# One run of probability-value matmuls per step instead of three, with scratch tiles shared

## The chip, the cores and the metric

The kernel runs on one core of a Trainium2 chip. The metric is the device time of one execution in microseconds (us), lower is better. The engines are named as the profile names them: PE is TensorE's matmuls, PEld its weight loads, DVE is VectorE, ACT is ScalarE, POOL is GpSimd, SP is the engine that issues the DMAs.

## The reference

Top-32 attention over 4 batches, 8 heads, 576 positions of 64 values, then two feed-forward layers over all 2304 tokens:

```
scores = (q @ k.T) / sqrt(64)                  # per batch and head, 576 x 576
scores = where(scores >= 32nd largest of the row, scores, -1e9)
attn   = softmax(scores) @ v                   # heads side by side: x, 2304 x 512
x = (sigmoid(x @ w_gate) * (x @ w_val)) @ w_out        # 512 -> 1536 -> 512
h = x @ w_in                                           # 512 -> 1024
out = layernorm(h * softmax(h)) * g_ln @ w_out2        # 1024 -> 512
```

All inputs are float32.

## The kernel before, in words

Attention is cut into 72 steps. 64 of them are main steps: 128 query rows of one head pair of one batch. 8 are remainder steps, which hold the last 64 rows of two head pairs. Four steps fill one chunk of 128 tokens (18 chunks), and each chunk then goes through the two feed-forward layers.

One step runs like this. TensorE makes the scores (`scores`, L607), ScalarE copies them out (L614), VectorE searches the top 32 with max and match-replace (L635, L639), ScalarE and GpSimd mask and exponentiate (L668, L672, L677), GpSimd scales the rows (L694). The probabilities then have to be turned: `flip` (L704) transposes the step's nine 128x128 blocks in three groups of 4, 4 and 1 blocks through the one PSUM tile with tag `pt`; `take_flip` (L711 for batch 0, L714 otherwise) copies a group to SBUF on ScalarE, and for batches 1 to 3 `rest_flip` (L719) writes the low half of the numbers on VectorE (tile `et`, two float16 parts). `attend` (L739) multiplies the group with the values: the stationary operand is a 128x64 block of values, the moving one 128 probabilities, and the output is one half (64 partitions) of the chunk's PSUM tile `av`. Batch 0 is done with one float32 matmul per block, the others with three float16 ones. A main step has 30 such float16 matmuls (12, 12 and 6 by group) or 10 float32 ones (4, 4 and 2 matmuls by program; the profile shows each float32 matmul as two instructions: 8, 8 and 4). All other matmuls of the kernel have a stationary operand of 128 columns.

The feed-forward layers of a chunk are `gate` and `value` (L886, 12 groups of 12 matmuls each), `down` (L932, 12 groups of 12), a norm (`norm2`, L938: ScalarE squares `px` into a scratch tile that nobody reads, only its sum is used), `hidden` (L969, 8 groups of 3 matmuls of 512 columns), layer norm, `turn` (L1041, transposes) and `last` (L1067, 8 groups of 3). Between them ScalarE writes a float32 copy of a result into a tile with tag `xf` (one buffer: `xf`, `xg`, `lf`, 64 times in all), and GpSimd reads it to make a low half (L778, L959, L1058).

At the start VectorE rebuilds the weights from 64-bit words (L411 to L418). For one matrix ScalarE squares its 12 pieces (`square`, L425, scratch tag `sq`). `norm_v` (L585) squares the 16 value tiles (scratch tag `sj`, which `norm2` uses too).

The order of all work on every engine is fixed before the kernel is emitted. Class `Order` holds operations with engine, cost, rank, needs and the buffers they take and free, and plays a list schedule with them; the rank of an operation is its due time plus the sums of `SHIFT` entries, a table of some 400 numbers. On the chip each engine runs its own list strictly in that order. `BUFS` says how many buffers each tag has. In the planner, one `at` operation stands for one call of `attend`, with costs of 0.36, 0.36 and 0.18 us for the three groups of a float16 step.

Of the kernel before, what the change touches and what calls it, by code (L numbers as in the profile page):

```python
# [43 lines left out]
BUFS = dict(s=4, ks=8, v=4, qr=3, qs=3, w=2, et=3, eu=2, ps=1, pt=1, av=1, pm=4, xt=1, gh=1, two=3, big=2, xf=1, sq=1, x2=1)  # L44
# [263 lines left out]
def body(ctx, tc, q_main, q_rem, k_dup, v_pad, w_gate, w_val, w_out1, w_in, w_out2, g_ln, out):  # L308
# [72 lines left out]
    def weights(key, dst, src, kk, nn, by_column=False, fold=None):  # L381
# [41 lines left out]
        def square(f, c):  # L423
            state["sq", f, c] = sq = tl(sp, [P, 512], BF16, "sq", "sq")
            nc.scalar.activation(sq, piece(f, c), AF.Square)  # L425
# [373 lines left out]
    for i, st in enumerate(steps):  # L799
# [49 lines left out]
        for g in parts:  # L849
# [5 lines left out]
            elif i and not st["first"]:  # L855
                needs.append(("at", i - 1, 2))
# [354 lines left out]
```

## Time and profile before

| | us |
|---|---|
| median of the runs (3) | 1113.74 |
| lowest and highest | 1113.10 and 1115.08 |
| the profiled execution's own time | 1114.34 |
| its span, first to last instruction | 1112.2 |
| mean granted TensorE clock in it | 0.958 |

The times of the steps come from the profiled execution, which took 2.1 us more than its span and 0.6 us more than the median. "Busy" of PE is modelled: matmuls overlap in the pipeline, so that what a group of matmuls costs is the distance from its start to the start of the next group.

### The profile page before, as it was taken

The numbers are of one execution on the slowest core, as the hardware profiler recorded it, in microseconds if no ns is written. First come the engines' busy times: TensorE is split into PE (matmuls) and PEld (weight loads), VectorE is DVE, ScalarE is ACT, GpSimd is POOL, SyncE is SP. The second block draws the span as 40 slices with busy tenths as digits, with TensorE's granted clock in tenths as the row PEclk, the third lists the DMA queues.
The fourth block names the chain that finished last, engine by engine and source line by source line (L and its number), as shares of the span: only waits on it lengthen the run. The fifth ranks groups of instructions, "written<-read, shape, count | busy, mean of one in ns | idle before, by whom it ended". The sixth has DMA issues, their size and how long they took to land.

```text
span 1112.2 us, 31341 instructions
## 1 busy us (share of the span) xinstructions
PE 984.1 (88%) x12500; PEld 796.3 (72%) x12500; DVE 977.8 (88%) x2888; ACT 826.1 (74%) x1561; POOL 701.1 (63%) x940
## 2 busy tenths in 40 slices
PE   1536837699999999999999999999999999999995
PEld 1324835488786877887878787887977797887962
DVE  8998999999799999998999999996999999995232
ACT  2697599977888877786889677778798786766331
POOL 3555487967887677668688675667687566564100
PEclk9975869899999999999999999999999999999998
DMA  9844331011220000012100000012200000000000
GB/s 323 282 133 161 103 129 54 1 35 42 79 73 17 16 12 26 22 48 59 57 32 9 23 12 21 25 38 89 68 16 11 26 12 6 12 11 11 2 11 19
DMA packets 29474, 59.16 MB, mean 53 GB/s; under 512 B 3984, under 2 KB 14224, under 8 KB 29328
## 3 DMA queue, kind: packets, MB, share of 16 engines
q1 hardware_dynamic: 29328, 57.16, 15.7%
q8 instruction: 98, 1.61, 0.6%
q14 instruction: 48, 0.39, 0.1%
HBM read 52.43 MB, written 4.72 MB: 51 GB/s over the span
## 4 chain that ended last, share of the span: by engine, by line
PE 55%; ACT 18%; DVE 15%; POOL 5%; DMA 4%; issue 3%; SPq 0%; POOLq 0%; ACTq 0%
PE pg L886 10%; PE px L932 9%; PE pv L886 8%; PE po L1067 7%; PE ph L969 6%; PE av L739 5%; DVE m L635 5%; PE pt L704 5%; PE ps L607 4%; DVE w L639 4%; DMA kr<-in_k_dup_dram 2%; ACT s L677 2%; ACT w L668 2%; ACT ts L472 2%; ACT s L614 1%
## 5 line engine op out<-in xcount | busy, mean ns | idle before, releaser
L635 DVE MAX8 m<-w 128x8 f32<-128x576 f32 (+1 forms) x576 | 338.6, 602 | 2.8
L639 DVE MATCH_REPLACE8 w<-m,w 128x288 f32<-128x288 f32 (+1 forms) x432 | 233.9, 543 | 0.0
L672 POOL TENSOR_TENSOR s<-s,w 128x576 f32<-128x576 f32 x144 | 203.3, 1419 | 40.3 <-ACT w L668 39.4
L932 PE MATMUL px<-gh,wo 128*128 128x128 f16 x2592 | 178.8, 220 | 0.5 <-POOL gh L920 0.5
L932 PEld LDWEIGHTS <-wo 128*128 128x128 f16 x2592 | 157.2, 99 | 24.0 <-issue 1.7
L886 PE MATMUL pg<-xt,wg 128*128 128x128 f16 x2592 | 169.0, 221 | 3.1 <-DVE jk L438 1.4
L886 PE MATMUL pv<-xt,wv 128*128 128x128 f16 x2592 | 166.5, 219 | 1.0 <-DVE wi L418 1.0
L886 PEld LDWEIGHTS <-wv 128*128 128x128 f16 x2592 | 151.7, 98 | 16.6 <-issue 2.3
L607 PE MATMUL ps<-ks,qs 128*128 128x288 f32 x640 | 129.1, 330 | 38.4 <-DVE w L625 18.9
L886 PEld LDWEIGHTS <-wg 128*128 128x128 f16 x2592 | 154.1, 99 | 11.5 <-issue 2.8
L668 ACT ACTIVATE w<-s,ed 128x576 f32<-128x576 f32 x144 | 120.4, 864 | 31.1 <-POOL ed L663 30.8
L607 PEld LDWEIGHTS ps<-ks,qs 128*128 128x128 f32 x640 | 96.4, 198 | 51.3 <-issue 14.5
L704 PE MATMUL pt<-ident,s 128*128 128x128 f32 x648 | 115.4, 287 | 15.2 <-ACT et L711 8.7
L969 PE MATMUL ph<-wi,x 128*128 128x512 f16 x432 | 122.4, 394 | 3.0 <-ACT x L949 2.2
L1067 PE MATMUL po<-wo,lt 128*128 128x512 f16 x432 | 120.8, 392 | 2.0 <-ACT lf L1050 2.0
L677 ACT ACTIVATE s<-s,nm 128x576 f32<-128x576 f32 x144 | 111.3, 774 | 14.0 <-POOL s L672 13.3
L714 ACT ACTIVATE et<-pt 128x512 f16<-128x512 f32 (+1 forms) x162 | 78.6, 485 | 53.7 <-PE pt L704 46.4
L614 ACT ACTIVATE s<-ps 128x576 f32<-128x576 f32 x144 | 93.0, 646 | 28.7 <-PE ps L607 25.5
L694 POOL TENSOR_SCALAR s<-s,sm 128x576 f32<-128x576 f32 x132 | 97.4, 746 | 24.7 <-DVE sm L686 17.6
L719 DVE SCALAR_TENSOR_TENSOR et<-pt,et 128x512 f16<-128x512 f32 (+1 forms) x162 | 89.0, 549 | 24.1 <-ACT et L714 23.2
L739 PE MATMUL av<-et,v 128*64 128x128 f16 (+3 forms) x2200 | 107.7, 234 | 0.6 <-ACT et L711 0.5
L704 PEld LDWEIGHTS pt<-ident,s 128*128 128x128 f32 x648 | 76.8, 145 | 40.7 <-ACT et L711 15.3
(179 smaller groups left out, 1668.5 us busy)
## 6 DMA issues: line engine op xcount, KB each, us to landing
kr<-in_k_dup_dram SPq DMA_DIRECT2D x16, 576.0 KB, 4.0
qr<-in_q_main_dram SPq DMA_DIRECT2D x64, 128.0 KB, 2.5
v<-in_v_pad_dram SPq DMA_DIRECT2D x16, 320.0 KB, 3.4
wi<-in_w_gate_dram SPq DMA_DIRECT2D x8, 512.0 KB, 5.2
wo<-in_w_val_dram SPq DMA_DIRECT2D x8, 512.0 KB, 6.3
raw<-in_w_in_dram SPq DMA_DIRECT2D x8, 512.0 KB, 3.7
wi<-in_w_out_dram SPq DMA_DIRECT2D x8, 512.0 KB, 4.3
raw<-in_w_out_dram SPq DMA_DIRECT2D x8, 512.0 KB, 3.3
```

Source lines behind the costliest of these rows:

```text
L607: nc.tensor.matmul(pt[:, nn, :S // 2], qs[:, hl, slot], ks[:, nn * (S // 2):(nn + 1) * (S // 2)], start=x == 0, stop=x == len(mm) - 1)
L635: nc.vector.max(st["m8"][:, t, r * 8:r * 8 + 8], ranked(i, r, t))
L639: nc.vector.match_replace(w, steps[i]["m8"][:, t, r * 8:r * 8 + 8], w, LOW)
L668: nc.scalar.activation(st["w"][:, t], st["s"][:, t], AF.Relu, bias=st["ed"][:, 1, t:t + 1], scale=st["ed"][:, 0, t:t + 1])
L672: nc.gpsimd.tensor_sub(st["s"][:, t], st["s"][:, t], st["w"][:, t])
L677: nc.scalar.activation(w, w, AF.Exp, bias=st["nm"][:, t:t + 1], scale=D ** -0.5, accum_out=st["sm"][:, t:t + 1])
L704: nc.tensor.transpose(pt[:, x], wf[:, k * P:(k + 1) * P], ident)
L739: nc.tensor.matmul(ch["av"][j * D:(j + 1) * D, p, st["o"]:st["o"] + wd], v, e[:, y * REM:y * REM + wd], start=one and k == (0, 5)[j], stop ...
L886: nc.tensor.matmul(dst, w[a][:, c, f * P:(f + 1) * P], ch["xt"][:, b, c], start=x == 0, stop=x == len(mm) - 1)
L932: nc.tensor.matmul(ch["px"][:, e], wo1h[a][:, f, e * P:(e + 1) * P], ch["gh"][:, b, f], start=y == 0, stop=y == len(DOWN) - 1)
L969: nc.tensor.matmul(ch["ph", nn], ch["x2"][:, a, c], wih[b][:, c, nn * 512:(nn + 1) * 512], start=c == 0 and a == 0 and b == 0, stop=c == K ...
L1067: nc.tensor.matmul(ch["po"], ch["lt"][:, a, f], wo2h[b][:, f], start=y == 0, stop=y == len(FIN) - 1)
```

## The change

`attend` is called once per step and multiplies all nine blocks, in the same order of blocks and terms as before. In the planner its operation needs all three groups of the step, and frees their buffers together; its cost is 1.06 us for a float16 main step. The first group of a step takes both `et` buffers of the step at once, and `et` grows from 3 buffers to 4. To make room, the scratch tags `sq` and `sj` go: `square` writes into the buffer of tag `x2` (one buffer, the input of `hidden`), `norm_v` and `norm2` into that of tag `xf`. The `SHIFT` table is replaced as a whole.

```diff
-BUFS = dict(s=4, ks=8, v=4, qr=3, qs=3, w=2, et=3, eu=2, ps=1, pt=1, av=1, pm=4, xt=1, gh=1, two=3, big=2, xf=1, sq=1, x2=1)
+BUFS = dict(s=4, ks=8, v=4, qr=3, qs=3, w=2, et=4, eu=2, ps=1, pt=1, av=1, pm=4, xt=1, gh=1, two=3, big=2, xf=1, x2=1)
...
-    ("m", "first"): -68.8, ("r", 0): 592.7, ("r", "first"): -187.5, ("m", 1): -2148.3, ("r", 1): -823.6,
...
+    ("m", "first"): -17.1, ("r", 0): 598.7, ("r", "first"): -174, ("m", 1): -2556.4, ("r", 1): -732.5, ("m", 2): 8.4,
...
-            state["sq", f, c] = sq = tl(sp, [P, 512], BF16, "sq", "sq")
+            state["sq", f, c] = sq = tl(sp, [P, 512], BF16, "sq", "x2")
...
-        sq = tl(sp, [P, NBLK + 1, D], BF16, "sqv", "sj", 1)
+        sq = tl(sp, [P, NBLK + 1, D], BF16, "sqv", "xf")
...
-    def attend(i, g):
+    def attend(i):
...
-        blocks = range(NBLK) if st["rem"] else range(4 * g, min(4 * g + 4, NBLK))
...
-                      for x in blocks for j in range(2)]
+                      for x in range(NBLK) for j in range(2)]
...
-                      for x0 in range(0, len(blocks), 2) for n, (a, c) in enumerate(TERMS) for x in blocks[x0:x0 + 2]
-                      for j in range(2)]
+                      for x0 in range(0, NBLK, 2) for n, (a, c) in enumerate(TERMS)
+                      for x in range(x0, min(x0 + 2, NBLK)) for j in range(2)]
...
-        add(("vn", b, p), "ACT", 0.75, t + STEP, lambda b=b, p=p: norm_v(b, p), [("vd", b, p)])
+        add(("vn", b, p), "ACT", 0.75, t + STEP, lambda b=b, p=p: norm_v(b, p), [("vd", b, p)], take=["xf"], free=["xf"])
...
-            add(("et", i, g), "ACT", (0.49, 0.49, 0.17)[g], e + 6, lambda i=i, g=g: take_flip(i, g), [("fl", i, g)], take=[ET[g]],
+            add(("et", i, g), "ACT", (0.49, 0.49, 0.17)[g], e + 6, lambda i=i, g=g: take_flip(i, g), [("fl", i, g)] + [("et", i, g - 1)] * (g > 0),
+                take=(["et"] * 2, [], ["eu"])[g],
...
-        parts = (2,) if rem else range(3)
-        for g in parts:
-            whole = b in WHOLE
-            needs = [("et" if whole else "ez", i, x) for x in (range(3) if rem else [g])]
...
+        whole = b in WHOLE
+        needs = [("et" if whole else "ez", i, x) for x in range(3)]
+        needs += [n for p in st["pairs"] for n in ([("vd", b, p)] if whole else [("vl", b, p, x) for x in range(2)])]
+        needs += [("at", i - 1)] * (i > 0 and not st["first"])
+        add(("at", i), "PE", 1.41 if whole else 1.18 if rem else 1.06, e + 6, lambda i=i: attend(i), needs,
+            take=["av"] if st["first"] else [],
+            free=list(ET) + ["v"] * sum(uses[b, p][-1] == i for p in st["pairs"]))
...
-        sq = tl(sp, [P, 512], BF16, "sq2", "sj", 1)
+        sq = tl(sp, [P, 512], BF16, "sq2", "xf")
...
-        op(("n2",), "ACT", 0.57, 43, lambda ch=ch: norm2(ch), [("do", x, 11)])
+        op(("n2",), "ACT", 0.57, 43, lambda ch=ch: norm2(ch), [("do", x, 11)], take=["xf"], free=["xf"])
```

## Rows read from the trace of the kernel before

**Rows 1.** The page, part 1: busy time of each engine, its share, instructions.

```profile
PE 984.1 (88%) x12500; PEld 796.3 (72%) x12500; DVE 977.8 (88%) x2888; ACT 826.1 (74%) x1561; POOL 701.1 (63%) x940
```

**Rows 2.** Busy time by stretch: us, each engine (instructions), PEclk, DMA share, GB/s.

```profile
0.00:200.00 200.00, 105.29 (x894) 80.31 (x894) 186.32 (x485) 150.58 (x253) 115.77 (x128) 0.82 0.49 165
200.00:350.00 150.00, 138.70 (x1771) 117.83 (x1772) 140.03 (x437) 124.33 (x243) 116.47 (x161) 0.98 0.14 44
350.00:1008.00 658.00, 649.48 (x8800) 532.28 (x8799) 619.81 (x1892) 514.00 (x1003) 457.74 (x634) 1.00 0.09 28
1008.00:1037.00 29.00, 29.00 (x383) 22.16 (x380) 8.83 (x18) 12.84 (x21) 4.84 (x7) 1.00 0.03 11
1037.00:1112.20 75.20, 61.59 (x662) 43.77 (x659) 22.80 (x60) 24.31 (x44) 6.30 (x12) 0.93 0.03 12
...
350.00:500.00 150.00, 149.33 (x2048) 121.66 (x2046) 145.09 (x448) 121.48 (x237) 104.63 (x149) 1.00 0.08 25
```

**Rows 3.** Groups by form, line 739: busy us, mean ns, idle before.

```profile
L739 PE MATMUL av<-et,v 128*64 128x128 f16 x1440 | 66.9, 224 | 0.0
...
L739 PEld LDWEIGHTS <-v 128*64 128x64 f16 x1800 | 50.7, 110 | 28.6 <-issue 20.3 <-ACT tv L592 0.4 <-ACT v L593 0.2
...
L739 PE MATMUL av<-et,v 128*64 128x128 f32 x320 | 31.1, 324 | 0.6 <-ACT et L711 0.5
```

**Rows 4.** TensorE's timeline near 1022 us: start, us, what, count.

```profile
1022.24 0.83 PE L886 MATMUL pv<-xt,wv 128*128 128x128 f16 x12
1023.00 0.53 PE L739 MATMUL av<-et,v 128*64 128x128 f16 x12
1023.46 0.84 PE L886 MATMUL pv<-xt,wv 128*128 128x128 f16 x12
1024.23 0.36 PE L739 MATMUL av<-et,v 128*64 128x128 f16 x6
1024.53 0.66 PE L704 MATMUL pt<-ident,s 128*128 128x128 f32 x4
...
1026.24 0.84 PE L886 MATMUL pv<-xt,wv 128*128 128x128 f16 x12
1026.92 0.84 PE L969 MATMUL ph<-wi,x 128*128 128x512 f16 x3
```

**Rows 5.** TensorE's timeline: one of the two runs of 24 matmuls.

```profile
734.62 0.86 PE L739 MATMUL av<-et,v 128*64 128x128 f16 x24
735.42 0.84 PE L886 MATMUL pg<-xt,wg 128*128 128x128 f16 x12
```

**Rows 6.** TensorE's timeline: first and last runs of line 739, float32, then float16.

```profile
205.94 1.10 PE L739 MATMUL av<-et,v 128*64 128x128 f32 x8
...
299.19 0.44 PE L739 MATMUL av<-et,v 128*64 128x128 f32 x4
...
371.19 0.53 PE L739 MATMUL av<-et,v 128*64 128x128 f16 x12
...
1037.12 0.36 PE L739 MATMUL av<-et,v 128*64 128x128 f16 x6
```

**Rows 7.** Waits of ScalarE, by cause: us in total, times, longest.

```profile
ACT et L714 <- PE av L739: 7.0, 4, 3.2
...
ACT xg L953 <- POOL lt L1058: 1.3, 2, 0.7
...
ACT lf L1050 <- POOL lt L1058: 0.8, 1, 0.8
```

**Rows 8.** Timelines of PE, DVE and ACT: four instructions, idle in brackets.

```profile
843.24 1.44 PE L886 MATMUL pg<-xt,wg 128*128 128x128 f16 x23 [0.69 <-POOL xt L778]
...
1008.24 0.15 DVE L657 TENSOR_SCALAR ed<-ed 128x1 uint32<-128x1 uint32 x1
...
1037.53 0.60 ACT L761 ACTIVATE xt<-av 128x512 f16<-128x512 f32 x1 [8.82 <-PE av L739]
...
1099.58 1.94 PE L1041 MATMUL pl<-ident,e 128*128 128x128 f32 x8 [8.10 <-DVE e L1033]
```

More of the change, by code (lines that the diff above doesn't have):

```diff
@@ L161, in terms @@
     own += [((k, "first"), 1.0)] * (name[1] < 18) + [((k, "end"), 1.0)] * (name[1] > 63)
-    return [((k, name[2]) if k in ("m", "r", "fl", "et", "ez", "at") else k, 1.0), (("A", name[1] // 4), 1.0)] + own
+    return [((k, name[2]) if k in ("m", "r", "fl", "et", "ez") else k, 1.0), (("A", name[1] // 4), 1.0)] + own
 class Order:
@@ L175 @@
     TAKER = dict(s="ACT", ks="POOL", v="DMA", qr="DMA", qs="POOL", w="DVE", et="ACT", eu="ACT", ps="PE", pt="PE", av="PE", pm="PE",
-                 xt="ACT", gh="ACT", two="ACT", big="DMA", xf="ACT", sq="ACT", x2="ACT")
+                 xt="ACT", gh="ACT", two="ACT", big="DMA", xf="ACT", x2="ACT")
     WINDOW, TABLE, FIRST, BACK = 3413, 1280, 1650, 150
@@ L489, in weights @@
             if by_column:
-                add(("wq", *W), "ACT", 0.52, t, lambda f=f, c=c: square(f, c), [("wr", *W)], take=["sq"])
+                add(("wq", *W), "ACT", 0.52, t, lambda f=f, c=c: square(f, c), [("wr", *W)], take=["x2"])
                 add(("wp", *W), "PE", 0.22, t, lambda f=f, c=c: columns(f, c),
-                    [("wq", *W)] + [("wp", key, f, c - 1)] * (c > 0), take=["pm"] if c == 0 else [], free=["sq"])
+                    [("wq", *W)] + [("wp", key, f, c - 1)] * (c > 0), take=["pm"] if c == 0 else [], free=["x2"])
                 if c == kk - 1:
@@ L847, in body @@
                 add(("ez", i, g), "DVE", (0.6, 0.6, 0.2)[g], e + 6, lambda i=i, g=g: rest_flip(i, g), [("et", i, g)], free=["pt"])
-        parts = (2,) if rem else range(3)
-        for g in parts:
-            whole = b in WHOLE
-            needs = [("et" if whole else "ez", i, x) for x in (range(3) if rem else [g])]
-            needs += [n for p in st["pairs"] for n in ([("vd", b, p)] if whole else [("vl", b, p, x) for x in range(2)])]
-            if g != parts[0]:
-                needs.append(("at", i, g - 1))
-            elif i and not st["first"]:
-                needs.append(("at", i - 1, 2))
-            add(("at", i, g), "PE", (1.35 if whole else 0.9) if rem else (0.69, 0.69, 0.46)[g] if whole else (0.36, 0.36, 0.18)[g], e + 6, lambda i=i, g=g: attend(i, g), needs,
-                take=["av"] if st["first"] and g == parts[0] else [],
-                free=list(ET if rem else ET[g:g + 1]) + ["v"] * (g == 2) * sum(uses[b, p][-1] == i for p in st["pairs"]))
+        whole = b in WHOLE
[5 more added lines that the diff above has]
+            free=list(ET) + ["v"] * sum(uses[b, p][-1] == i for p in st["pairs"]))
         if st["last"]:
@@ L867, in body @@
                           free=["pt"])
-            needs = [("at", i, 2), ("ve", key)]
+            needs = [("at", i), ("ve", key)]
             for bb in ch["vs"]:
```

142 rows, old and new, of the table SHIFT are left out of this document.

## The prediction

> **What bounds the kernel now.** I read the page first: over the whole span TensorE and VectorE are busy alike, 88% each [rows 1], so the average names no bound. The table of stretches does more [rows 2]. Up to 200 us TensorE is busy for 105 of 200 us while VectorE is for 186: there VectorE sets the pace (it rebuilds weights and searches the first top 32). From 350 to 1008 us TensorE is busy for 649.5 of 658 us, with a granted clock of 1.00: it idles 8.5 us, VectorE 38.2 us. The top-32 search ends at 1008.2 us [rows 8]. In the 29 us behind it TensorE has no idle time at all, and in the last 75.2 us it is busy for 61.6 [rows 2], the largest hole being the 8.1 us before the last transposes [rows 8]. So TensorE works off a queue from 350 us on, and that queue is still there when the search is over. The sign of this is ScalarE's wait of 8.8 us at 1037.5 us for the last run of `av` matmuls [rows 8]: other matmuls stood before it in TensorE's list. A microsecond taken from TensorE after 350 us should thus shorten the kernel, as long as VectorE can follow.
>
> **What a run of `av` matmuls costs.** The listed busy times don't say it, since matmuls overlap: line 739 shows 224 ns for one float16 matmul [rows 3]. I take distances between starts in the timeline [rows 4]. A group of 12 `pv` matmuls followed by other full-width matmuls takes 0.68 us (1026.24 to 1026.92). The same group followed by `av` takes 0.76 or 0.77 us (1022.24 to 1023.00, 1023.46 to 1024.23): entering the run costs 0.09, say 0.10. A run of 12 `av` matmuls takes 0.46 us to the next start, a run of 6 takes 0.30. The difference of 6 matmuls is 0.16 to 0.17, or 0.028 each, so 12 matmuls are 0.34 and 0.12 us is left that depends on no matmul: leaving the run. A run of 24 confirms the line: 0.80 us [rows 5] against 24 x 0.028 + 0.12 = 0.79. So every run costs 0.22 us on top of its matmuls. The weight loads show the same from their side: 28.6 us of idle time before those of line 739, mostly under "issue", which is no wait for another engine [rows 3].
>
> **Part 1, one run instead of three.** The matmuls stay: 1440 of float16 in main steps, 320 of float32 [rows 3]. Only runs go. Between the first and the last run of the float16 main steps [rows 6] I counted 139 runs, without the remainder steps' (48 steps x 3, less 5 places where two already stand together). After it 48 are left: 91 x 0.22 = 20.0 us of TensorE's time. Bounds: 10.9 if a merged run still pays the entering somewhere (91 x 0.12), 20.9 at 0.23 per run, the top of the readings. A merged run of 30 comes to 0.10 + 0.84 + 0.12 = 1.06 us; before, the three are 0.56 + 0.56 + 0.40 = 1.52.
>
> The float32 steps after 200 us have 26 runs [rows 6] for 10 steps: 16 x 0.22 = 3.5 us at the most. TensorE is not full there (138.7 of 150 us from 200 to 350 [rows 2]), so I take half, 1.8; lower bound 0, upper 3.5. Before 200 us I take nothing: TensorE idles half of that time, and VectorE's 186 us cover it. The remainder steps are one run already and stay.
>
> **How much of it arrives.** VectorE's 619.8 us from 350 to 1008 [rows 2] don't shrink. Its fullest long stretch, 350 to 500 us, is 145.1 of 150, or 96.7% [rows 2]. At that share the 658 us can become 619.8 / 0.967 = 641, so the search could end 17 us earlier. The rest can come out of the tail: a chunk's own groups on TensorE are 36 of about 0.67 us and 16 of about 0.68 [rows 4], 35 us, of the 61.6 busy behind 1037 us; some 26 us there are older chunks' work. Both routes together hold more than 20 us. Against that, TensorE waits a dozen times between 350 and 1008 us, the last cluster ending at 843.2 us [rows 8], where it had caught up; time saved just before such a wait is lost in it. My estimate is that 85% of 21.8 arrives: 18.5 us.
>
> A rule of the Trainium skill (Perfetto Trace Analysis, Identifying the Most-Contended Engine) speaks against this. It says that matmul busy time is no measure of TensorE's load and that the busy share of weight loads is to be taken. By it TensorE stands at 532.3 / 658 = 81% from 350 to 1008 us [rows 2], VectorE at 94% would be the most contended, and the sum would be that of the first rival below. The timeline agrees with it only that the busy figure is padded; starts that follow each other without a gap show a full list.
>
> **Part 2, buffers.** Three `et` buffers become four, taken in pairs. ScalarE waits for `av` matmuls to free an `et` 4 times for 7.0 us now [rows 7]. A pair is held until the step's one run, but two steps fit instead of one and a half; I take 0, between -7 (those waits go) and +3.2 (one more of the longest). The run now comes after the third group's low half, so 30 instead of 6 matmuls stand behind the last group of a chunk: 24 x 0.028 = 0.7 us later for ScalarE's copy. This is covered by other chunks' matmuls except at the last chunk, so I charge 0.7 once; without that cover it would be 18 chunks, 12 us.
>
> **Part 3, shared scratch.** `square` takes the buffer of `x2`, which nobody needs before the first chunk's second layer: 0. `norm_v` (16 times) and `norm2` (18 times) now need the single `xf`, so ScalarE may stand until GpSimd has read the copy before. Behind it on ScalarE wait the score copies and `et` copies, and for those wait TensorE and VectorE. Today's 64 users of `xf` wait 1.3 + 0.8 = 2.1 us altogether [rows 7], 0.033 each; 34 more give 1.1 us, of which I let 0.2 through, since ScalarE is busy for only 514 of 658 us [rows 2]. Bounds: 0, and 34 x 0.7 (the longest such wait) = 24 us.
>
> **Part 4, the replaced table.** It moves work on all queues, DMA issues on SP's included, by amounts that the trace of before cannot show. I take 0; the bounds are what order alone can give or take: the 8.5 us in which TensorE idles from 350 to 1008 us [rows 2], gained or doubled.
>
> Sum on the profiled execution's 1114.3: -18.5 + 0.7 + 0.2 = -17.6, or 1096.7. The median of the runs is 0.6 lower, so 1096.
>
> **The rivals.** First, VectorE sets the pace: attention doesn't speed up, TensorE only idles longer up to the cluster of waits that ends at 843 us, and what counts is saved behind it. By then 16 of the 48 steps are left, with 46 runs: 30 x 0.22 = 6.6 us, or 1107. For it speaks VectorE's 94%; against it that VectorE idles 38 us in that stretch and that the queue outlives the search. Chance 0.20. The rule of the Trainium skill named above (Perfetto Trace Analysis) would have it this way.
>
> Second, the gain is eaten at each step: the merged run sits in TensorE's list where VectorE's third low half isn't done, and waits some 0.4 us per step (48 x 0.4 = 19). Today TensorE hardly waits at `av`: 0.6 us of idle at its float32 runs, 0.0 at the float16 ones [rows 3]. 1113.7; chance 0.09.
>
> Third, slower: `xf`. The place is ScalarE's squares at L938 and L585. Each stands until GpSimd has finished the copy before. It decides against the change when the 34 waits cost the path over 0.52 us each (17.6 / 34). At the longest wait seen, 0.7, it is 24 - 17.6, about 6 us above: 1120. Against it: the same buffer causes 0.033 us per use now [rows 7]. Chance 0.13, in which I include the replaced table going wrong at the batch changes at the same price.
>
> **Numbers.** The forecast has 0.58, with its own range of 1088 to 1103. A change of 0.2% (2.2 us) is about what the runs can tell from none. Faster by more: 0.58 + 0.20 = 0.78; within: 0.09; slower: 0.13. The range takes the forecast and the first rival. Its lower end is all of 20.0 + 3.5, and some 5 of the idle time or of the `et` waits: 1114.3 - 29 = 1085. Its upper end is 1110, the first rival with only 4 us left.
>
> **What would show it.** Right: 48 float16 runs of 30 with 0.95 to 0.97 us from their start to the next, TensorE still above 97% from 350 us to the end of the search, the search ending before 1000 us, and VectorE at 96% or more. Wrong: the search still ending near 1008 us with more TensorE idle (first rival); idle time before `av` for VectorE's low halves (second); ScalarE's squares waiting for GpSimd by tens of microseconds (third). The forecast fails as a whole if a merged run costs more per matmul than 0.028.

## The result, and the profile after

| | before | after |
|---|---|---|
| median of the runs, us | 1114.41 | 1099.56 |
| lowest to highest, us | 1113.10 to 1117.45 | 1097.92 to 1101.90 |
| the profiled execution: time, span, us | 1114.34, 1112.2 | 1101.90, 1100.1 |

The ratio is 0.9864, with a 95% interval of 0.9836 to 0.9893: 14.9 us faster. A second measurement of the changed kernel, beside the last experiments, gave 1099.91 us and 0.9869 (0.9851 to 0.9888). The profiled execution of after is the slowest of its four runs.

Part 1 of the page of the changed kernel, busy time of each engine:

```profile
PE 970.6 (88%) x12500; PEld 801.8 (73%) x12500; DVE 971.5 (88%) x2888; ACT 827.8 (75%) x1561; POOL 701.2 (64%) x940
```

Again both shares are 88%, as in [rows 1], and again they name no bound. By line and form, line 738 (739 before), with busy us, mean ns and the idle time in front:

```profile
L738 PE MATMUL av<-et,v 128*64 128x128 f16 x1440 | 49.2, 221 | 0.0
...
L738 PEld LDWEIGHTS <-v 128*64 128x64 f16 x1800 | 48.0, 110 | 10.1 <-issue 7.0 <-POOL v L597 0.3
```

Their count is that of [rows 3] and their mean about the same, but TensorE is busy with them for 17.7 us less, and the idle time before their weight loads fell from 28.6 to 10.1 us: 18.5 us, close to the 20.0 that the prediction had counted from 91 runs. In the timeline 139 runs became 46, so 93 went: 44 runs of 30 matmuls are left, and two of 60, where two steps stand together. One of the two, and one of the 44 between its neighbours (start, us, what, count):

```profile
380.20 1.87 PE L738 MATMUL av<-et,v 128*64 128x128 f16 x60
...
444.61 0.84 PE L881 MATMUL pv<-xt,wv 128*128 128x128 f16 x12
445.39 1.03 PE L738 MATMUL av<-et,v 128*64 128x128 f16 x30
446.35 0.66 PE L704 MATMUL pt<-ident,s 128*128 128x128 f32 x4
```

The group of 12 in front takes 0.78 us to the run's start (0.67 where no run follows), and the run of 30 takes 0.96 us to the next start. The median over such runs is 0.96.

The stretches, cut at the new end of the search (us, busy PE, PEld, DVE, ACT, POOL, with instruction counts, then PEclk, DMA share, GB/s):

```profile
200.00:350.00 150.00, 142.63 (x1800) 121.11 (x1799) 138.16 (x440) 130.98 (x252) 119.73 (x158) 0.98 0.13 42
350.00:993.00 643.00, 630.28 (x8721) 527.74 (x8720) 614.11 (x1886) 509.95 (x994) 455.09 (x634) 1.00 0.10 29
993.00:1025.00 32.00, 32.00 (x465) 25.46 (x462) 9.70 (x19) 12.84 (x23) 6.85 (x9) 1.00 0.03 10
1025.00:1100.00 75.00, 62.57 (x644) 43.63 (x640) 22.16 (x57) 25.55 (x45) 6.31 (x12) 0.93 0.03 12
```

To be read against [rows 2]: from 350 us to the end of the search TensorE idles 12.7 us (8.5 before) and VectorE 28.9 (38.2 before). The search's last instruction, ScalarE's first copy of the last chunk's `av`, and the last transposes, idle time in brackets:

```profile
992.93 0.15 DVE L657 TENSOR_SCALAR ed<-ed 128x1 uint32<-128x1 uint32 x1
...
1025.11 0.60 ACT L760 ACTIVATE xt<-av 128x512 f16<-128x512 f32 x1 [9.02 <-PE av L738]
...
1087.57 1.94 PE L1036 MATMUL pl<-ident,e 128*128 128x128 f32 x8 [6.73 <-DVE e L1028]
```

The search ends 15.3 us earlier than in [rows 8]. What follows did not get shorter: 107 us from there to the end of the span, 104 before. The copy still waits 9.0 us for `av`, the last transposes 6.7 us (8.8 and 8.1 in [rows 8]). So the whole gain was made before the search ended, and none in the tail.

The chain of work that ended last, by engine. First the kernel before, then the changed one:

```profile
PE 55%; ACT 18%; DVE 15%; POOL 5%; DMA 4%; issue 3%; SPq 0%; POOLq 0%; ACTq 0%
```

```profile
DVE 32%; PE 31%; ACT 20%; POOL 9%; DMA 5%; issue 3%; POOLq 0%; SPq 0%; DVEq 0%; ACTq 0%
```

TensorE went from more than half of the chain to a third, level with VectorE.

### The profile page after: what moved, and what is told of

Its sections match the earlier page's. It is cut to its first block, busy times and chain, and to the rows that moved or that the text cites. A ratio compares the mean times of both kernels' runs of the same rounds, so it can differ in the third digit from the quotient of the medians.

```text
span 1100.1 us, 31341 instructions
## 1 busy us (share of the span) xinstructions
PE 970.6 (88%) x12500; PEld 801.8 (73%) x12500; DVE 971.5 (88%) x2888; ACT 827.8 (75%) x1561; POOL 701.2 (64%) x940
## 4 chain that ended last, share of the span: by engine, by line
DVE 32%; PE 31%; ACT 20%; POOL 9%; DMA 5%; issue 3%; POOLq 0%; SPq 0%; DVEq 0%; ACTq 0%
DVE m L635 9%; DVE w L639 7%; PE px L927 6%; PE pg L881 5%; PE ph L964 4%; PE pv L881 4%; PE po L1062 4%; DVE et L719 3%; PE pt L704 3%; ACT w L668 2%; ACT s L677 2%; PE ps L607 2%; POOL s L672 2%; DVE pd L415 2%; DVE pd L411 2%
## 5 line engine op out<-in xcount | busy, mean ns | idle before, releaser
L881 PEld LDWEIGHTS <-wv 128*128 128x128 f16 x2592 | 155.3, 99 | 15.6 <-issue 0.7
L714 ACT ACTIVATE et<-pt 128x512 f16<-128x512 f32 x162 | 78.9, 487 | 48.1 <-PE pt L704 47.4
L719 DVE SCALAR_TENSOR_TENSOR et<-pt,et 128x512 f16<-128x512 f32 x162 | 89.0, 549 | 18.4 <-ACT et L714 17.8
L738 PE MATMUL av<-et,v 128*64 128x128 f16 (+3 forms) x2200 | 87.0, 234 | 0.2 <-POOL v L597 0.2
```

The lines of the kernel that those rows point to most:

```text
L719: nc.vector.scalar_tensor_tensor(et[:, 1], st["pt", g][:, :et.shape[2]], 1.0, et[:, 0], op0=OP.mult, op1=OP.subtract)
L881: nc.tensor.matmul(dst, w[a][:, c, f * P:(f + 1) * P], ch["xt"][:, b, c], start=x == 0, stop=x == len(mm) - 1)
```

## The experiments

Each ratio is against the kernel before, timed beside it on the same chip: 1116.97 us beside the merged runs in the old order, both kernels with two inserted matmuls per run and the three runs with the replaced table, 1115.53 beside the kernels with one engine relieved, 1114.72 beside the others. These are three chips. A difference in us between two kernels of different groups is thus one between chips; it rests on the changed kernel taking about the same on two of them (1099.91 us, and 1099.88 with the narrow inserts).

**The changed kernel again.** Same code.

> The changed kernel once more, as the base for the other runs: 1098 to 1101.

Measured: 1099.91 us.

**Merged runs in the old order.** Table, order and buffers of before; a group's matmuls are held back to the third group's place where no `et` buffer is missing. `EARLY_RUNS` lists the 37 groups, as (step, group), that can't wait for it.

```diff
     def attend(i, g):
...
+        if not st["rem"]:
+            st.setdefault("due", []).append(g)
+            if g < 2 and (i, g) not in EARLY_RUNS:
+                return
...
-        blocks = range(NBLK) if st["rem"] else range(4 * g, min(4 * g + 4, NBLK))
+        blocks = range(NBLK) if st["rem"] else [x for y in st.pop("due") for x in range(4 * y, min(4 * y + 4, NBLK))]
```

> The kernel before, with its table, its order on every engine and its buffers; only the matmuls of a step's earlier groups are moved to the place of the third group (or the second) wherever an et buffer allows it. 65 of the 91 float16 runs that the change removes go, and 26 float32 ones. If the gain is the price of entering and leaving a run: 65 x 0.22 = 14.3 us less for TensorE from 350 us on, and at the share that arrived in the change (15 of 20) about 11 us, so 1103. If the gain comes from the replaced table or the buffers: 1114, or slower, since the matmuls come later than planned.

Measured: 1114.54 against 1116.97 us, ratio 0.998 (0.9959 to 1.0001). No gain clear of noise: by itself this is the second theory's outcome. The counts in the expectation, 65 and 26, are of calls of `attend`; calls that stand together make one run, and in the timeline 139 float16 runs became 79 (60 fewer) and 39 float32 ones 21. The timeline also shows where to look, the first remainder run of batch 0 in the kernel before and in this one:

```profile
316.04 1.39 PE L739 MATMUL av<-et,v 128*64 128x64 f32 x40
```

```profile
324.49 1.39 PE L745 MATMUL av<-et,v 128*64 128x64 f32 x40
```

This profile is 8.4 us behind when batch 0 ends, in the part where the float32 runs were moved. So the next run leaves these alone.

**The same, float16 runs only.**

```diff
-        if not st["rem"]:
+        if not st["rem"] and st["b"] not in WHOLE:
             st.setdefault("due", []).append(g)
...
-        blocks = range(NBLK) if st["rem"] else [x for y in st.pop("due") for x in range(4 * y, min(4 * y + 4, NBLK))]
+        blocks = range(NBLK) if st["rem"] else [x for y in st.pop("due", [g]) for x in range(4 * y, min(4 * y + 4, NBLK))]
```

> The kernel before with its order, its table and its buffers; float16 runs moved together as in the first experiment (65 runs fewer, 14.3 us of TensorE), the float32 runs of batch 0 left as they were. In the first experiment the profile was 8 us behind when batch 0 was done. If moving the float32 runs cost that: -7 to -10 against before, as 13.4 us fewer of matmul time gave -9.4. If a late run costs as much as the fewer runs save, or the gain needs the replaced table: 0 to -3, as in the first experiment.

Measured: 1108.14 against 1114.72 us, 0.9946 (0.9927 to 0.9965): -6.6 us, a little short of the -7 to -10 expected. The timeline again has 79 float16 runs, 60 fewer, and nothing is changed but the place of these matmuls. The same run of batch 0 is back where it was:

```profile
315.95 1.39 PE L745 MATMUL av<-et,v 128*64 128x64 f32 x40
```

So fewer runs alone make the kernel faster, by 0.50 us for each of the 13.2 us (60 x 0.22) that TensorE is spared. Why the moved float32 runs cost some 4 us was not tested. ScalarE's waits up to 310 us for `av` matmuls to free an `et`, in the kernel before and in the one with both kinds moved, point at the late runs (us, times, longest):

```profile
ACT et L711 <- PE av L739: 2.3, 1, 2.3
```

```profile
ACT et L711 <- PE av L745: 5.2, 3, 2.3
```

**Runs broken up again, in the new order.** Two inserted matmuls per float16 run, of full width. `zero` is a tile of zeros, so they add nothing to the result.

```diff
+            for x, (k, j, v, e, one, end) in enumerate(mm):
+                if x in (24, 48) and not st["rem"] and st["b"] not in WHOLE:
+                    nc.tensor.matmul(ch["av"][0:128, p, 0:1], zero[:, 0:128], e[:, 0:1], start=False, stop=False)
```

> The changed kernel with its order; in each float16 run of 30 two matmuls are inserted, between the groups, with a stationary operand of 128 zero columns and one moving column, so that the run is left and entered again twice (96 times in all). If a run costs 0.22 us on top of its matmuls: 96 x (0.22 + some 0.05 of its own) = 26 us more for TensorE, and 15 to 26 us more in all, 1115 to 1125. If the fewer runs are not what made the change faster: 96 x 0.05 = 5 us at most, 1100 to 1104.

**The control, 64 columns wide.** `ch["av"][0:64, p, 0:1]` and `zero[:, 0:64]` in the same place.

> Control for the one before: the same 96 inserted matmuls at the same places, but with 64 zero columns, the width of the run's own, so that the run is not left. 96 x 0.03 to 0.05 = 3 to 5 us of TensorE's time, 1100 to 1104 by either theory. If it is as slow as the wide one, what counts is an inserted instruction, not the change of width.

Measured: 1111.51 us with the wide ones (0.9951, 0.9929 to 0.9973), 1099.88 with the narrow ones (0.9849, 0.9824 to 0.9875). The same step in TensorE's timeline, wide and then narrow:

```profile
457.16 0.53 PE L742 MATMUL av<-et,v 128*64 128x128 f16 x12
457.62 0.18 PE L740 MATMUL av<-et,zero 128*128 128x1 f16 x1
457.73 0.53 PE L742 MATMUL av<-et,v 128*64 128x128 f16 x12
458.19 0.18 PE L740 MATMUL av<-et,zero 128*128 128x1 f16 x1
458.30 0.36 PE L742 MATMUL av<-et,v 128*64 128x128 f16 x6
458.59 0.85 PE L968 MATMUL ph<-wi,x 128*128 128x512 f16 x3
```

```profile
454.47 0.53 PE L742 MATMUL av<-et,v 128*64 128x128 f16 x12
454.83 0.17 PE L740 MATMUL av<-et,zero 128*64 128x1 f16 x1
454.83 0.55 PE L742 MATMUL av<-et,v 128*64 128x128 f16 x13
455.19 0.17 PE L740 MATMUL av<-et,zero 128*64 128x1 f16 x1
455.22 0.33 PE L742 MATMUL av<-et,v 128*64 128x128 f16 x5
455.49 0.85 PE L968 MATMUL ph<-wi,x 128*128 128x512 f16 x3
```

From the run's start to the next group it is 1.43 us with the wide ones and 1.02 with the narrow ones: 0.41 us per step, 48 x 0.41 = 19.7 us of TensorE's time. An inserted narrow matmul costs its 0.03 us (1.02 against 0.96 for two) and nothing else. It is the change of width that costs, and putting it back gives back 11.6 us of the 14.9. The size was below what I expected (15 to 26 us), since only 0.59 of each microsecond shows. The chain that ended last goes back to TensorE too, 50% of it with the wide ones (55% in the kernel before, 31% in the changed one):

```profile
PE 50%; DVE 19%; ACT 16%; POOL 7%; DMA 6%; issue 2%; POOLq 0%; SPq 0%; ACTq 0%; DVEq 0%
```

**Four breaks per run.** `x in (12, 24, 36, 48)`.

> The changed kernel with four full-width matmuls in each float16 run instead of two: another 20 us of TensorE's time on top of the 20 that gave 11.6. If TensorE bounds the kernel fully once it has that much more work: +16 to +20 over the two-breaker kernel, 1128 to 1132. If other engines hide a constant share: +11 to +12, 1123.

Measured: 1126.43 us, ratio 1.0108 (1.0087 to 1.0129), 14.9 us more than with two, between the two expectations. A run's first two and its last piece, and the next group:

```profile
457.80 0.36 PE L742 MATMUL av<-et,v 128*64 128x128 f16 x6
458.09 0.18 PE L740 MATMUL av<-et,zero 128*128 128x1 f16 x1
...
459.40 0.36 PE L742 MATMUL av<-et,v 128*64 128x128 f16 x6
459.69 0.85 PE L968 MATMUL ph<-wi,x 128*128 128x512 f16 x3
```

From the run's start to the next group it is 1.89 us. Each pair of wide matmuls thus adds about the same, 0.46 to 0.47 us per step or some 22 us in all (0.96, 1.43, 1.89); the first pair cost 11.6 us (0.52 of each of these 22; of the 19.7 against the narrow ones it was 0.59) and the second 14.9 (0.67). The share rises as TensorE has more to do. Set against the kernel before beside each, whose time differed by 2.2 us, the second step would be 17.2 us; it is larger than the first either way. TensorE's stretch from 350 to 980 us with two breaks, then four (columns as above):

```profile
350.00:980.00 630.00, 622.63 (x8520) 519.65 (x8519) 597.13 (x1827) 495.69 (x967) 446.14 (x618) 1.00 0.09 29
```

```profile
350.00:980.00 630.00, 626.20 (x8461) 519.80 (x8459) 586.09 (x1785) 487.60 (x949) 435.10 (x604) 1.00 0.09 29
```

TensorE's idle time falls from 7.4 to 3.8 us.

**Three runs with the replaced table.** `attend` and its operations as before, buffers and table of the changed kernel, planned anew.

> Three runs per step as before, planned anew with the replaced table and with the buffers of the changed kernel (four et in pairs, shared scratch). If the gain is that of the fewer runs: 1110 to 1125, since a table made for other costs need not fit. If the table or the buffers bring the gain: about 1100.

Measured: 1159.78 us, ratio 1.04 (1.0373 to 1.0428), far above both expectations. The table and the buffers bring no gain by themselves; the table belongs to one set of operations. How much it adds with the merged run is not separated by this. The merged kernel with the old table was not run.

**TensorE or VectorE relieved, before and after.** Two terms instead of three (the result is less exact), and a shorter last round of the search (it looks at half of a row, so the result is another one). The cuts of code are of the changed kernel; `n == 2` becomes `n == 1` with the first:

```diff
-                      for x0 in range(0, NBLK, 2) for n, (a, c) in enumerate(TERMS)
+                      for x0 in range(0, NBLK, 2) for n, (a, c) in enumerate(TERMS[:2])
```

```diff
+        w = st["w"][:, t, :S // 2] if (r, t) == (3, 0) else ranked(i, r, t)
-        nc.vector.max(st["m8"][:, t, r * 8:r * 8 + 8], ranked(i, r, t))
+        nc.vector.max(st["m8"][:, t, r * 8:r * 8 + 8], w)
```

> The kernel before, same order; the third of the three float16 products is left out of the probabilities times the values (the result is less exact): 480 matmuls of 0.028 us, 13.4 us less for TensorE, the runs stay 139. If a microsecond of TensorE's time is worth a microsecond: -11 to -13. If the fixed order lets little through, as when the runs were merged in the old order: -1 to -4.

> The kernel before, same order; the last round of the top-32 search looks at half of the row for one of the two heads (the result is another one): 72 x 0.30 = 21.6 us less for VectorE, nothing else. If TensorE alone bounds the kernel before: 0 to -3 us. If VectorE paces it beside TensorE: -6 to -14 us. VectorE alone: -18 or more.

> The same cut of 13.4 us of TensorE's work in the changed kernel, against 1099.6. By the widened runs in this order (20 us of TensorE gave 11.6): -6 to -8 us. If VectorE now bounds: 0 to -3.

> The same cut of 21.6 us of VectorE's work in the changed kernel, to be read against 1099.6. If the change has made VectorE the bound: -12 to -20 us. If both engines hold each other by the fixed order: -4 to -12, about as in the kernel before. TensorE alone: 0 to -3.

> The changed kernel with both cuts at once, two terms (13.4 us of TensorE) and the shorter last search (21.6 us of VectorE). Alone they gave -1.5 and -4. If each engine holds the other: clearly more than the sum, -9 to -14. If something else paces the kernel now, the single buffers between the engines or ScalarE and GpSimd: about the sum, -4 to -7.

| | before | after |
|---|---|---|
| TensorE 15.3 us less | -9.4 (1106.09 of 1115.53) | -1.8 (1098.08 of 1099.91) |
| VectorE 18.0 us less | -2.2 (1113.29 of 1115.53) | -4.6 (1095.32 of 1099.91) |
| both | | -4.2 (1095.73 of 1099.91) |

The sizes are those of the traces. The expectations' 13.4 us left out the six float16 remainder runs, which shrink too (1.08 to 0.76 us each, 1.9 us); and where 72 searches of 0.30 us less make 21.6, VectorE's busy time as a whole fell by 18.0 us in both kernels.

In the kernel before, TensorE's time counted (9.4 of 15.3, 0.61 of each microsecond) and VectorE's hardly did (2.2 of 18.0, 0.12). In the changed one neither counts much: -1.8 us is hardly clear of the noise and misses the -6 to -8 expected, -4.6 is at the low end of what was expected if the engines hold each other, and both together give no more than VectorE alone. So the expectation for the pair that each engine holds the other up fell; -4.2 us is what was expected if something else paces the kernel. The stretch from 350 to 980 us of the changed kernel, then of that with two terms:

```profile
350.00:980.00 630.00, 617.31 (x8563) 517.11 (x8561) 601.41 (x1847) 500.93 (x976) 447.92 (x623) 1.00 0.09 29
```

```profile
350.00:980.00 630.00, 606.60 (x8020) 502.95 (x8019) 602.98 (x1852) 499.26 (x978) 448.76 (x623) 1.00 0.10 29
```

TensorE is busy 10.7 us less and simply idles: 12.7 us become 23.4. What it waits for, in the kernel before, in the changed one and then with two terms (us, times, longest):

```profile
PE pt L704 <- DVE et L719: 2.5, 4, 1.6
```

```profile
PE pt L704 <- DVE et L719: 7.6, 13, 2.1
PE ps L607 <- DVE w L625: 1.1, 4, 0.4
```

```profile
PE pt L704 <- DVE et L719: 11.5, 17, 1.7
PE ps L607 <- DVE w L625: 1.9, 6, 0.6
```

The transposes wait for VectorE's low halves, which release the single `pt` tile. With both cuts TensorE still idles 21.9 us, and VectorE's work is smaller:

```profile
350.00:980.00 630.00, 608.12 (x8050) 505.28 (x8048) 594.93 (x1863) 502.22 (x985) 450.77 (x628) 1.00 0.09 29
```

The chain that ended last is then led by ScalarE:

```profile
ACT 29%; DVE 25%; PE 24%; POOL 13%; issue 4%; DMA 4%; POOLq 0%; SPq 0%; ACTq 0%; DVEq 0%
```

So neither engine's load alone paces the kernel now, nor the two together. That it is steps of one engine behind another in a fixed order, with the single `pt` tile as the tightest, is read from the waits and not shown: ScalarE and GpSimd were not relieved, and a second `pt` tile was not tried.

## Why the prediction was right, point by point

**What bounds the kernel before**: right. It rested on a full list for TensorE, and the two relieved kernels show it: 15.3 us of TensorE gave 9.4, 18.0 us of VectorE gave 2.2. The first rival said that VectorE sets the pace; the same runs refute it. With it fell the rule of the Trainium skill (Perfetto Trace Analysis, Identifying the Most-Contended Engine) as applied here: TensorE's weight loads were 81% busy and VectorE 94%, and still TensorE was the one to relieve. The section names the share of the peak arithmetic beside the weight loads; that was not worked out here.

**The cost of a run**: right, 0.22 us. Predicted 0.95 to 0.97 us for a run of 30, measured 0.96; two breaks cost 0.41 us per step more than two inserts of the run's own width. The Trainium skill (TensorEngine Tiling (Array Packing), Key Properties) has a rule for it: changing the tiling mode drains the engine. The trace agrees in that a 64-column matmul inserted in a 64-column run costs 0.03 us and a 128-column one 0.2 more; that the time goes into a drain can't be seen in it.

**TensorE's time saved**: 20.0 predicted from 91 float16 runs, 18.5 by the idle time of the weight loads; 93 runs went. Giving back 19.7 us of it took back 11.6 of the gain; in the old order, 60 runs fewer (13.2 us) gave 6.6. So the fewer runs carry most of the gain in the new order, and no single share of it holds for both orders. The remaining 3 us of 14.9 (float32 runs, buffers, the replaced table) are not told apart, so that part of the agreement is not explained by the mechanism that was forecast. For the float32 runs I had put 1.8 us. The trace has 25 of them after 200 us, not 26, and nothing saved can be seen when batch 0 ends: its first remainder run, at 316.04 us in the kernel before, stands here in the changed one:

```profile
318.00 1.39 PE L738 MATMUL av<-et,v 128*64 128x64 f32 x40
```

**How much arrives**: the term that was mis-sized. I let 85% of 21.8 us through, and 14.9 of 21.8 is 68%. There is no constant share: in the changed kernel's order a microsecond of TensorE's time is worth 0.67 from 22 us above its load, 0.52 in the first 22, and 0.12 below it (1.8 of 15.3). The change brought the kernel to where TensorE's time nearly stops counting. The sum had only its 85% for this; that less arrived for this reason fits these runs. The two routes were wrong in their split as well: VectorE's 96.7% was taken as a ceiling and it reached 95.5%, while the tail, which I thought would give some of the gain, gave none. The order of the last chunks kept the last `av` runs 31 us behind the search.

**Buffers**: ScalarE's four waits for `av` to free an `et` [rows 7] are gone from its list of waits; I had left these 7 us out of the sum, and what they brought is among the 3 us not told apart. For `xf`, no wait of the squares at L585 and L933 for GpSimd shows at all. The third rival had its place there; it did not happen. Its price was misread: the longest wait in [rows 7] is 0.8 us, not 0.7, which makes 34 x 0.8 = 27 us and 1123, not 1120. The second, a wait of the merged run for VectorE, did not happen either: line 738 has 0.0 us of idle time at its float16 main-step runs. But TensorE does wait longer for VectorE's low halves at the transposes, 7.6 us against 2.5 from 350 to 980 us: the second rival's cause at another place, at 5 us instead of 19.

**The signs named**: runs of 30 at 0.96 (44 of them and two of 60, where 48 were named), TensorE at 98.0% (630.28 of 643), the search ending at 993 us came as said; VectorE at 96% or more did not quite (95.5%).

## What to carry to other kernels

Count how often a matmul stream changes between 64 and 128 stationary columns, and read its price from start-to-start distances at the change: here 0.22 us per visit, which the mean time of one matmul (224 ns before, 221 after) does not show. Before spending more on the engine that binds, relieve each candidate by a cut that leaves the order alone, in the kernel before and in the new one: the same 15 us of TensorE were worth 9.4 and then 1.8. A table of due times tuned for one set of operations is part of that set; with the other set, and the changed buffers, the kernel was 4% slower than before.

## What the runs showed of the hardware that was not expected

Two matmuls with 64 stationary columns that fill opposite halves of the output take together as long as one with 128: where the halves alternate, 12 more matmuls of 128 moving columns in a run take 0.34 us (0.028 each, from runs of 12 and 24), and 12 with 128 columns take 0.67 (0.056 each). A 128-column matmul of one moving column inside such a run costs 0.2 us more than a 64-column one. At 0.056 us for a 128-column matmul in a row of its like, most of that is for the two changes of width.
